# A recurrence-to-expert kernel: constants moved from GpSimd to ScalarE in the opening, more filler matmuls, one bonus product on VectorE

## The chip, the core and the metric

The kernel runs on one core of a Trainium2 chip. The metric is the device time of one execution in microseconds, as the median of several runs. The profile is a separate execution, taken by the hardware profiler; its rows give times from the start of its span. Engines: PE is TensorE (matmul; PEld is its weight load), DVE is VectorE, ACT is ScalarE, POOL is GpSimd, SP is SyncE, which here issues most transfers. TensorE's clock has two levels, 2.4 GHz (shown as a granted clock of 1.00) and 1.2 GHz (0.50).

## What is computed

First a linear recurrence for 4 batches, 8 heads, 768 positions and head size 48, then one of 8 experts for each batch, chosen from the mean of that batch's recurrence output:

```python
for t in range(S):
    cur = einsum('bhd,bhe->bhde', u * k[t], v[t])
    y[t] = einsum('bhd,bhde->bhe', r[t], state + cur)
    state = w * state + einsum('bhd,bhe->bhde', k[t], v[t])
x = y as (B, S, 384)
logits = x.mean(axis=1) @ w_gate ; e = argmax(logits) per batch
out[b] = softmax(logits)[e] * (relu(x[b] @ w1[e]) @ w2[e])
```

## The kernel before

The sequence is cut into 12 blocks of 256 positions, numbered g = 0 to 11, three to a batch. Each block goes through the same steps, and the order of the steps is written out by hand (`manual_schedule`): every engine executes its instructions in the order in which the program text emits them. Two decays are built once from `w` (`dk`, `dr`). For a block, `load(g)` starts three transfers of 384 KB (k, r, v) on SP's queue. `prep_k` and `prep_r` scale k and r by the decays into bf16 (block 0 on VectorE, all others on GpSimd); `prep_v` casts v to bf16 (ScalarE for blocks 0 to 3). `transposes(g, c)` turns k and r round on TensorE in two halves; after each half ScalarE copies the result from PSUM (`kr`, L243) and VectorE forms the product of k and r (`prod`, L244). `scores(g, 0)` and `scores(g, 1)` multiply k with r into one PSUM tile `at`, which VectorE masks into `gt` (L265); there is one buffer of `at`, so the next scores step waits for that masking. `bonus(g)` sums `prod` against the constant `U8` into 16 columns of the PSUM bank `s_ps`, VectorE copies them out (`tcol`, L288), and GpSimd multiplies v by them (`vt`, L296). `scores_v(g, 1, ..)` and `scores_v(g, 0, ..)` multiply `gt` with v into the outputs `ys`, and k with v into the running state in `s_ps`; VectorE then reads that state out with a mask (`st`, L367): with `bmask` after the half-block step, with `wcmask` after the whole block. `inter(g, j)` adds the carried state's part to the output, `add_bonus(g)` adds `vt`, `evac_y(g, j)` lets ScalarE cast the output to `xn` (L380), and `backs(g)` transposes it back (`xp`, L393), sums it over positions into `s_ps` (L397), and ScalarE copies it to `xt` (L401). `outputs(g)` is the run of these from `inter(g, 0)` to `backs(g)`.

The first three blocks (the opening) are ordered one step at a time in the lines from L551 on. After block 2, `pool_sum(0)`, `gate(0)` and `weights(0)` find the expert of batch 0 and GpSimd issues the transfers of its weights (L453, L457). From block 3 on, a loop interleaves the recurrence with jobs of the expert of the batch before (`mm1`, L474, and `mm2`, L494); the first such job comes at the end of block 3. `fill(n, cols)` issues n matmuls on a tile of zeros, whose result nobody reads, and `gap()` is `fill(1, 256)`.

The tile framework adds the waits. For the PSUM bank `s_ps` a later write waits for an earlier read of the same tile. The constants that the change touches are built ahead of all blocks: `wuT` holds w and u by partition (four small transfers on ScalarE's queue, each half filling 48 of 64 partitions); GpSimd squares w eight times (`wpow`, L182) and multiplies the mask by it (`wcmask`, L185), ahead of its scaling of block 1.

Of the kernel before, what the change touches and what calls it, by code (L numbers as in the profile page):

```python
# [9 lines left out]
FP32 = mybir.dt.float32  # L10
FP32R = mybir.dt.float32r
BF16 = mybir.dt.bfloat16
AX = mybir.AxisListType
ALU = mybir.AluOpType
ACT = mybir.ActivationFunctionType
# [3 lines left out]
def kernel(  # L19
# [12 lines left out]
    nc = tc.nc  # L32

    B, H, S, D = r.shape
    DM = H * D
    C = 128
    L = 2 * C
    DP = 64
    NP = H // 2
# [11 lines left out]
    const = ctx.enter_context(tc.tile_pool(name="const", bufs=1))  # L51
    inp = ctx.enter_context(tc.tile_pool(name="inp", bufs=AHEAD))
    work = ctx.enter_context(tc.tile_pool(name="work", bufs=4))
# [18 lines left out]
    def load(g):  # L72
        b, gi = divmod(g, NB)
        for name, src in (("k32", k), ("r32", r), ("v32", v)):
            t = inp.tile([128, H, 2, D], FP32, tag=name, name=f"{name}_{g}")
            nc.sync.dma_start(
                out=t.rearrange("q h c d -> q h (c d)"),
                in_=src[b, :, L * gi : L * gi + L, :].rearrange("h (q c) d -> q h (c d)", c=2),
            )
            raw[name, g] = t  # L80
# [7 lines left out]
    nc.sync.dma_start(out=wrow, in_=w.rearrange("(o h) d -> o (h d)", o=1))  # L88

    wuT = const.tile([128, 2, NP], FP32, tag="wuT", name="wuT")  # L90
    nc.vector.memset(wuT, 0.0)
    with nc.allow_non_contiguous_dma(reason="decay and bonus by partition, 1.5 KB each"):
        for i, src in enumerate((w, u)):
            for a in range(2):
                nc.scalar.dma_start(
                    out=wuT[64 * a : 64 * a + D, i, :],
# [14 lines left out]
    def fill(cnt, cols):  # L111
        for _ in range(cnt):
            nc.tensor.matmul(out=fills[-1][:, 0:cols], lhsT=zero[:, 0:128],  # L113
                             rhs=zero[:, 0:cols], start=True, stop=True)
# [60 lines left out]
    for a in range(2):  # L175
        q = slice(64 * a, 64 * a + 64)
        nc.gpsimd.tensor_mul(
            U8.rearrange("q p h -> q (p h)")[q, a :: H + 2], wuT[q, 1, :], wuT[q, 0, :])
    wpow = [wuT[:, 0, :]]
    while 2 ** (len(wpow) - 1) < L:  # L180
        t = const.tile([128, NP], FP32, tag=f"wpow{len(wpow)}", name=f"wpow{len(wpow)}")
        nc.gpsimd.tensor_mul(t, wpow[-1], wpow[-1])  # L182
        wpow.append(t)
    wcmask = const.tile([128, NP, 2 * D], FP32, tag="wcmask", name="wcmask")
    nc.gpsimd.tensor_mul(  # L185
        wcmask, bmask.rearrange("q p a d -> q p (a d)"),
        wpow[-1].to_broadcast([128, NP, 2 * D]))
    ones_col = const.tile([128, 1], BF16, tag="ones_col", name="ones_col")
    nc.vector.memset(ones_col, 1.0)

# [11 lines left out]
    def prep_k(g):  # L202
        kg, rg = raw.pop(("k32", g)), raw[("r32", g)]
        if g == 0:
            for c in (c0, c1):
                scale(nc.vector, kp[g % NR], kg, dk, c)
                scale(nc.vector, rp[g % NR], rg, dr, c)
        else:
            scale(nc.gpsimd, kp[g % NR], kg, dk, cc)
# [6 lines left out]
    def prep_v(g):  # L216
        vb = work.tile([128, 2, H, D], BF16, tag="vb", name=f"vb{g}")
        vsrc = raw.pop(("v32", g)).rearrange("q h c d -> q c h d")
        if g < NB + 1:
            nc.scalar.copy(vb, vsrc)  # L220
        else:
            nc.gpsimd.tensor_copy(vb, vsrc)
        vbs[g] = vb

    def transposes(g, c):
        if c and g < NB + 2:
            fill_bank()
            twp = pp_moe.tile([128, 2 * NP, 128], BF16, tag="moe", name=f"twp{g}_{c}")
        else:
            twp = pp_tw.tile([128, 2 * NP, 128], BF16, tag="tw", name=f"twp{g}_{c}")  # L230
        for o, src in ((0, kp[g % NR]), (NP, rp[g % NR])):
            for p in range(NP):
                nc.tensor.transpose(  # L233
                    out=twp[:, o + p, :],
                    in_=src[:, c, 2 * p : 2 * p + 2, :].rearrange("s a b -> s (a b)"),
                    identity=ident,
                )
        if c == 0:
            kts[g] = work.tile([128, 2 * NP, 2, 2, 64], BF16, tag="kr", name=f"kr{g}")
            rts[g] = kts[g][:, NP : 2 * NP]  # L240
            prods[g] = work.tile([128, NP, 2, 2, 64], BF16, tag="prod", name=f"prod{g}")
        tw = twp.rearrange("q o (j i) -> q o j i", j=2)
        nc.scalar.copy(kts[g][:, :, :, c, :], tw)  # L243
        nc.vector.tensor_mul(prods[g][:, :, c], tw[:, 0:NP], rts[g][:, :, :, c, :])  # L244

    def scores(g, rnd):
        kt, rt = kts[g], rts[g]
        if rnd == 0:
            gts[g] = work.tile([128, 2, 2, 2, 2, 128], BF16, tag="gt", name=f"gt{g}")
        at = pp_at.tile([128, 2, 2, 2, 128], FP32, tag="at", name=f"at{g}_{rnd}")  # L250
        for pp in range(2):
            p = 2 * rnd + pp
            for cs in range(2):
                for j in range(2):
                    for a in range(2):
                        q = slice(64 * a, 64 * a + D)
                        nc.tensor.matmul(  # L257
                            out=at[64 * j : 64 * j + 64, a, pp, cs, :],
                            lhsT=kt[q, p, j, cs, :],
                            rhs=rt[q, p, j].rearrange("q c i -> q (c i)"),  # L260
                            start=True,
                            stop=True,
                            skip_group_check=True,
                        )
        nc.vector.tensor_mul(  # L265
            gts[g][:, rnd].rearrange("q a p c t -> q (a p) c t"),
            at.rearrange("q a p c t -> q (a p) c t"),
            mask.rearrange("q n s c i -> q n s (c i)"),
        )
# [3 lines left out]
    def bonus(g, now=True):  # L273
        prod = prods[g]
        if g:
            tc_ps = s_ps[(g - 1) // NB][:, TC : TC + 2 * H]
        else:
            tc_ps = pp_y.tile([128, 512], FP32, tag="y0", name="tc0")[:, 0 : 2 * H]
        for c in range(2):
            for p in range(NP):  # L280
                nc.tensor.matmul(
                    out=tc_ps[:, H * c : H * c + H],
                    lhsT=prod[:, p, c].rearrange("q j i -> q (j i)"), rhs=U8[:, p, :],
                    start=(g == 0 and c == 0 and p == 0), stop=(p == NP - 1),
                    skip_group_check=True,
                )
        tcol = work.tile([128, 2 * H], FP32, tag="tcol", name=f"tcol{g}")
        nc.vector.tensor_copy(tcol, tc_ps)  # L288
        tcols[g] = tcol
        if now:  # L290
            vt_mul(g)
# [8 lines left out]
    def inter(g, j):  # L300
        st, rt = sts.pop((g, j)), rts[g]
        yj = ys[g][j]
        for p in range(NP):
            nc.tensor.matmul(  # L304
                out=yj[:, 96 * p : 96 * p + 96],
                lhsT=rt[:, p, j].rearrange("q c i -> q (c i)"), rhs=st[:, p, :],
                start=(j == 0 and p == 0), stop=False, skip_group_check=True,
            )

    def add_bonus(g):  # L310
        vt = vts[g].rearrange("q (c h) d -> q c (h d)", c=2)
        for j, c in ((0, 0), (1, 1), (0, 1), (1, 0)):
            q = slice(64 * j, 64 * j + 64)
            nc.tensor.matmul(  # L314
                out=ys[g][j][64 * c : 64 * c + 64, 0:DM], lhsT=ident[q, q], rhs=vt[q, c, :],
                start=False, stop=True, skip_group_check=True,
            )
# [59 lines left out]
    def evac_y(g, j):  # L377
        if j == 0:
            xns[g] = work.tile([128, 2, DM], BF16, tag="xn", name=f"xn{g}")
        nc.scalar.copy(xns[g][:, j, :], ys[g][j][:, 0:DM])  # L380
# [151 lines left out]
    def outputs(g, gaps=None):  # L532

        gaps = gaps or [lambda: None] * 3
        if g % NB:
            inter(g, 0)
        scores_v(g, 0, g % NB == 0)
        add_bonus(g)
        evac_y(g, 0)
        gaps[0]()  # L540
        inter(g, 1)
        evac_y(g, 1)
        gaps[1]()
        backs(g)
        gaps[2]()

    def gap():
        fill(1, 256)
# [7 lines left out]
    scores(0, 0)  # L556
    prep_v(0)
    load(4)
    fill(5, 512)
    scores(0, 1)  # L560
    bonus(0, False)
# [4 lines left out]
    scores_v(0, 1, True)  # L566
    prep_v(1)
    load(5)
    fill(4, 256)
    scores(1, 0)  # L570
    scores_v(0, 0, True)
    fill(2, 256)
    scores(1, 1)
    bonus(1)
    prep_k(3)
    transposes(2, 0)
    transposes(2, 1)
    prep_v(2)
    add_bonus(0)
    evac_y(0, 0)  # L580
    inter(0, 1)
    evac_y(0, 1)
    gap()
    scores(2, 0)
    scores_v(1, 1, True)
    backs(0)
    gap()
    scores(2, 1)
    bonus(2)
    prep_r(3)  # L590
    outputs(1, [gap] * 3)
    prep_v(3)
    prep_k(4)
    scores_v(2, 1, True)
    outputs(2, [gap] * 3)
    pool_sum(0)
# [92 lines left out]
```

## Time and profile before

| | us |
|---|---|
| median of 3 runs (159.16 to 160.34) | 159.63 |
| the profiled execution, its own time | 161.36 |
| its span, first to last instruction | 159.7 |
| its mean granted TensorE clock | 0.904 |
| PE busy | 146.1 (91%) |
| DVE busy | 74.1 (46%) |
| ACT busy | 82.5 (52%) |
| POOL busy | 72.3 (45%) |

The profiled execution took 161.36 us, of which 1.66 lie outside its span. Busy shares are averages over stages with different limits: the opening lasts until about 37 us, the expert of batch 0 is found and its weights are asked for by 43 us, and its first matmul runs at 52 us. A busy TensorE is not one at its peak, because at 1.2 GHz the same work shows as busy for longer.

### The profile page before, as it was taken

How to read it: one execution, taken by the hardware profiler on the slowest of the kernel's cores; microseconds unless marked ns; L12 is line 12 of the kernel's file. 1: busy time of each engine (PE TensorE's matmuls, PEld its weight loads, DVE VectorE, ACT ScalarE, POOL GpSimd, SP SyncE). 2: the span in 40 equal slices, each digit the busy share in tenths (PEclk: the TensorE clock that was granted, in tenths of full speed). 3: DMA queues.
4: the chain of work that ended last, by engine and by line, in shares of the span. 5: the costliest groups of instructions: out<-in, count | busy, mean ns of one | idle time of the engine just before them, and what ended most of it. 6: DMA issues, size and time to landing. Idle time of an engine off the chain costs nothing.

```text
span 159.7 us, 4549 instructions
## 1 busy us (share of the span) xinstructions
PE 146.1 (91%) x1954; PEld 103.0 (64%) x1954; DVE 74.1 (46%) x164; ACT 82.5 (52%) x138; POOL 72.3 (45%) x72
## 2 busy tenths in 40 slices
PE   6984997798598999999999999999999999999991
PEld 2344676567376787777667877776677765676560
DVE  7863556311655655465545744665274321212110
ACT  1860645255326477654657686553764652265321
POOL 4089944750499492928839193592203020000000
PEclk9998559555559999999999999999999999999999
DMA  3999999700099999999999100299420039970034
GB/s 76 253 261 259 265 234 268 171 4 0 16 233 217 263 255 249 258 272 258 218 222 355 69 4 0 27 208 192 176 99 4 0 43 215 147 290 0 2 141 155
DMA packets 41464, 25.47 MB, mean 160 GB/s; under 512 B 38755, under 2 KB 39012, under 8 KB 41444
## 3 DMA queue, kind: packets, MB, share of 16 engines
q1 hardware_dynamic: 39460, 18.89, 47.3%
q0 software_dynamic: 1152, 6.29, 20.7%
q8 instruction: 15, 0.25, 0.7%
q10 hardware_dynamic: 832, 0.00, 0.3%
q14 instruction: 5, 0.04, 0.1%
HBM read 26.76 MB, written 4.72 MB: 197 GB/s over the span
## 4 chain that ended last, share of the span: by engine, by line
PE 73%; ACT 7%; DVE 6%; POOL 6%; DMA 3%; issue 2%; ACTq 1%; POOLq 1%
PE op L494 20%; PE hp L474 20%; PE twp L233 6%; PE y L344 5%; PE at L257 4%; DMA wuT<-in_u_dram 3%; PE s L352 3%; PE xp L393 3%; ACT kr L243 2%; PE fill L113 2%; POOL rp L196 2%; DVE gt L265 2%; PE y L304 2%; PE y L314 2%; ACT ht L481 2%
## 5 line engine op out<-in xcount | busy, mean ns | idle before, releaser
L474 PE MATMUL hp<-xt,w 128*128 128x384 bf16 x192 | 41.4, 333 | 1.3 <-DVE lg L427 0.3
L243 ACT COPY kr<-twp 128x1024 bf16<-128x1024 bf16 x24 | 24.0, 1012 | 24.1 <-PE twp L233 24.1
L494 PE MATMUL op<-w,ht 128*128 128x384 bf16 x192 | 34.9, 326 | 0.1
L265 DVE TENSOR_TENSOR gt<-at,mask 128x1024 bf16<-128x1024 f32 x24 | 29.3, 1222 | 10.1 <-PE at L257 9.9
L481 ACT ACTIVATE ht<-hp 128x384 bf16<-128x384 f32 x48 | 23.4, 491 | 17.7 <-PE hp L474 17.1
L296 POOL TENSOR_TENSOR vt<-vb,tcol 128x768 bf16<-128x768 bf16 x12 | 17.7, 1477 | 28.2 <-DVE tcol L288 28.2
L474 PEld LDWEIGHTS <-w 128*128 128x128 bf16 x192 | 25.1, 148 | 8.1 <-issue 4.4
L244 DVE TENSOR_TENSOR prod<-twp,kr 128x512 bf16<-128x512 bf16 x24 | 10.2, 425 | 30.9 <-ACT kr L243 30.9
L494 PEld LDWEIGHTS <-ht 128*128 128x128 bf16 x192 | 17.3, 98 | 11.1 <-issue 0.8
L196 POOL TENSOR_TENSOR rp<-r,dr 128x768 bf16<-128x768 f32 x11 | 20.0, 1818 | 0.0
L196 POOL TENSOR_TENSOR kp<-k,dk 128x768 bf16<-128x768 f32 x11 | 20.0, 1815 | 0.0
L113 PE MATMUL fill<-zero 128*128 128x256 bf16 (+1 forms) x48 | 15.6, 432 | 1.3 <-DVE zero L85 1.3
L344 PEld LDWEIGHTS <-gt 64*128 64x128 bf16 x384 | 12.6, 98 | 6.0 <-issue 5.1
L501 ACT ACTIVATE ob<-op,gw 128x384 f32<-128x384 f32 x16 | 9.3, 581 | 13.1 <-PE op L494 12.9
L344 PE MATMUL y<-vb,gt 64*128 64x48 bf16 x384 | 15.3, 188 | 0.6 <-ACT xn L380 0.6
L380 ACT CAST xn<-y 128x384 bf16<-128x384 f32 x24 | 11.3, 480 | 5.9 <-PE y L314 4.9
L483 DVE TENSOR_SCALAR ht<-hp 128x384 bf16<-128x384 f32 x16 | 8.9, 554 | 11.7 <-PE hp L474 11.5
L257 PE MATMUL at<-kr 48*64 48x128 bf16 x384 | 11.1, 240 | 3.0 <-ACT kr L243 1.5
L453 POOL DMA_DIRECT2D w<-in_moe_w_dram x4 | 2.5, 623 | 22.9 <-DVE gw L443 8.3
L257 PEld LDWEIGHTS <-kr 48*64 48x64 bf16 x384 | 7.6, 116 | 7.9 <-issue 6.6
L233 PE MATMUL twp<-ident,rp 128*128 128x128 bf16 x96 | 11.2, 250 | 1.4 <-POOL rp L196 1.4
L352 PE MATMUL s<-vb,kp 64*128 64x96 bf16 x160 | 11.7, 222 | 0.8 <-DVE tcol L288 0.8
(72 smaller groups left out, 162.8 us busy)
## 6 DMA issues: line engine op xcount, KB each, us to landing
w<-in_moe_w_dram POOLq DMA_DIRECT2D x8, 768.0 KB, 9.8
k<-in_k_dram SPq DMA_DIRECT2D x12, 384.0 KB, 6.2
r<-in_r_dram SPq DMA_DIRECT2D x12, 384.0 KB, 6.4
v<-in_v_dram SPq DMA_DIRECT2D x12, 384.0 KB, 6.3
out_dram<-ob SPq DMA_DIRECT2D x11, 384.0 KB, 4.8
out_dram<-ob SPq DMA_DIRECT2D x2, 192.0 KB, 1.9
wuT<-in_w_dram ACTq DMA_DIRECT2D x2, 0.8 KB, 3.6
wuT<-in_u_dram ACTq DMA_DIRECT2D x2, 0.8 KB, 4.7
```

Source lines behind the costliest of these rows:

```text
L113: nc.tensor.matmul(out=fills[-1][:, 0:cols], lhsT=zero[:, 0:128], rhs=zero[:, 0:cols], start=True, stop=True)
L196: eng.tensor_mul(dst[:, cs, :, 0:D].rearrange("q c h d -> q h c d"), src[:, :, cs, :], dec[:, :, cs, :])
L233: nc.tensor.transpose(out=twp[:, o + p, :], in_=src[:, c, 2 * p : 2 * p + 2, :].rearrange("s a b -> s (a b)"), identity=ident,)
L243: nc.scalar.copy(kts[g][:, :, :, c, :], tw)
L257: nc.tensor.matmul(out=at[64 * j : 64 * j + 64, a, pp, cs, :], lhsT=kt[q, p, j, cs, :], rhs=rt[q, p, j].rearrange("q c i -> q (c i)"), sta ...
L265: nc.vector.tensor_mul(gts[g][:, rnd].rearrange("q a p c t -> q (a p) c t"), at.rearrange("q a p c t -> q (a p) c t"), mask.rearrange("q n ...
L296: nc.gpsimd.tensor_mul(vt, vbs[g].rearrange("q c h d -> q (c h) d"), tcol.to_broadcast([128, 2 * H, D]))
L344: nc.tensor.matmul(out=yj[:, D * h : D * h + D], lhsT=gt[q, p // 2, a, p % 2, c, :], rhs=vb[q, c, h, :], start=(first and i == 0), stop=(c ...
L352: nc.tensor.matmul(out=sp[:, 96 * p : 96 * p + 96], lhsT=kp[g % NR][qo, c, 2 * p : 2 * p + 2, :].rearrange("s a b -> s (a b)"), rhs=vb[qo, ...
L474: nc.tensor.matmul(out=hp[:, 0:SB], lhsT=w1[:, ct, ft::NFT], rhs=xts[b][:, ct, SB * sb : SB * sb + SB], start=(ct == 0), stop=(ct == NCT - 1),
L481: nc.scalar.activation(out=o, in_=hp[:, 0:SB], func=ACT.Relu)
L494: nc.tensor.matmul(out=op[:, 0:DM], lhsT=ht[:, ft, 128 * si : 128 * si + 128], rhs=w2[:, ft, :], start=(ft == 0), stop=(ft == NFT - 1),)
```

## The change

The eight squarings and the masked product leave GpSimd. ScalarE computes w to the power 256 as exp(256 ln w) with two small activations in the place of the squarings, and writes `wcmask` with four scaled copies after it has cast v of block 0. The unused partitions of `wuT` are filled with 0.5 in place of 0, so that the logarithm stays finite. `bonus(g, None)` is a new form: VectorE multiplies v by the sums straight from PSUM, with no `tcol` and no work on GpSimd; block 2 uses it. The order of the opening changes: the first half of the transposes of block 2 comes ahead of `scores(1, 1)`; the outputs of block 1 are spread round `scores(2, 1)` and come ahead of `bonus(2)`; fillers are of other counts and widths, and most of the gaps leave.

```diff
-    nc.vector.memset(wuT, 0.0)
+    nc.vector.memset(wuT, 0.5)
...
-    wpow = [wuT[:, 0, :]]
-    while 2 ** (len(wpow) - 1) < L:
-        t = const.tile([128, NP], FP32, tag=f"wpow{len(wpow)}", name=f"wpow{len(wpow)}")
-        nc.gpsimd.tensor_mul(t, wpow[-1], wpow[-1])
-        wpow.append(t)
+    lnwT = const.tile([128, NP], FP32, tag="lnwT", name="lnwT")
+    nc.scalar.activation(out=lnwT, in_=wuT[:, 0, :], func=ACT.Ln)
+    wcT = const.tile([128, NP], FP32, tag="wcT", name="wcT")
+    nc.scalar.activation(out=wcT, in_=lnwT, func=ACT.Exp, scale=float(L))
     wcmask = const.tile([128, NP, 2 * D], FP32, tag="wcmask", name="wcmask")
-    nc.gpsimd.tensor_mul(
-        wcmask, bmask.rearrange("q p a d -> q p (a d)"),
-        wpow[-1].to_broadcast([128, NP, 2 * D]))
+
+    def late_constants():
+        for p in range(NP):
+            nc.scalar.activation(
+                out=wcmask[:, p, :], in_=bmask[:, p].rearrange("q a d -> q (a d)"),
+                func=ACT.Copy, scale=wcT[:, p : p + 1])
...
+        if now is None:
+            vts[g] = work.tile([128, 2 * H, D], BF16, tag="vt", name=f"vt{g}")
+            nc.vector.tensor_mul(
+                vts[g], vbs[g].rearrange("q c h d -> q (c h) d"),
+                tc_ps.to_broadcast([128, 2 * H, D]))
+            return
         tcol = work.tile([128, 2 * H], FP32, tag="tcol", name=f"tcol{g}")
...
     load(4)
+    late_constants()
     fill(5, 512)
...
     load(5)
-    fill(4, 256)
+    fill(3, 512)
     scores(1, 0)
     scores_v(0, 0, True)
-    fill(2, 256)
+    transposes(2, 0)
+    fill(1, 512)
     scores(1, 1)
     bonus(1)
     prep_k(3)
-    transposes(2, 0)
     transposes(2, 1)
     prep_v(2)
+    fill(2, 512)
     add_bonus(0)
     evac_y(0, 0)
     inter(0, 1)
     evac_y(0, 1)
-    gap()
     scores(2, 0)
     scores_v(1, 1, True)
     backs(0)
     gap()
+    inter(1, 0)
+    scores_v(1, 0, False)
     scores(2, 1)
-    bonus(2)
+    add_bonus(1)
+    evac_y(1, 0)
+    inter(1, 1)
+    evac_y(1, 1)
+    bonus(2, None)
     prep_r(3)
-    outputs(1, [gap] * 3)
     prep_v(3)
     prep_k(4)
+    backs(1)
+    gap()
     scores_v(2, 1, True)
```

## Rows read from the trace of the kernel before

**Rows 1.** Five stretches of TensorE: length, busy (instructions), granted clock, DMA share, GB/s.

```profile
12.40:15.10 2.70, 0.70 (x15) 0.87 1.28 259
15.10:24.60 9.50, 9.41 (x148) 0.50 1.17 250
25.50:28.05 2.55, 2.35 (x66) 1.00 1.19 289
28.05:48.50 20.45, 17.31 (x226) 0.50 0.40 88
52.10:159.70 107.60, 102.57 (x1356) 1.00 0.63 153
```

**Rows 2.** The chain that ended last, parts: start, length, what.

```profile
8.48 0.21 POOL wpow L182
...
10.69 0.79 POOL wcmask L185
...
15.10 1.46 PE twp L233 x12
...
52.14 0.64 PE hp L474 x3
```

**Rows 3.** Timeline of POOL: start, length, what, idle time before it.

```profile
13.24 1.80 POOL L196 TENSOR_TENSOR rp<-r,dr 128x768 bf16<-128x768 f32 x1
...
16.76 1.82 POOL L196 TENSOR_TENSOR rp<-r,dr 128x768 bf16<-128x768 f32 x1
18.54 1.48 POOL L296 TENSOR_TENSOR vt<-vb,tcol 128x768 bf16<-128x768 bf16 x1
...
42.24 0.72 POOL L453 DMA_DIRECT2D w<-in_moe_w_dram x1 [8.26 <-DVE gw L443]
```

**Rows 4.** DMA issues at 5.10, 9.66, 10.13; last column, us to landing.

```profile
r<-in_r_dram SPq DMA_DIRECT2D x1, 384.0 KB, 6.3
...
k<-in_k_dram SPq DMA_DIRECT2D x1, 384.0 KB, 4.9
...
r<-in_r_dram SPq DMA_DIRECT2D x1, 384.0 KB, 5.9
```

**Rows 5.** Timeline of ACT: two pairs of copies and the nearest small activation.

```profile
8.28 1.93 ACT L243 COPY kr<-twp 128x1024 bf16<-128x1024 bf16 x2 [0.74 <-PE twp L233]
...
15.74 1.93 ACT L243 COPY kr<-twp 128x1024 bf16<-128x1024 bf16 x2 [4.81 <-PE twp L233]
...
40.73 0.30 ACT L439 ACTIVATE exps<-lg,negmax 128x8 f32<-128x8 f32 x1 [1.09 <-DVE negmax L437]
```

**Rows 6.** Groups by form, 4 to 60 us: count, busy us, mean ns, idle before.

```profile
L265 DVE TENSOR_TENSOR gt<-at,mask 128x1024 bf16<-128x1024 f32 x11 | 13.5, 1224 | 4.1 <-PE at L257 4.0
...
L296 POOL TENSOR_TENSOR vt<-vb,tcol 128x768 bf16<-128x768 bf16 x5 | 7.4, 1475 | 7.9 <-DVE tcol L288 7.9
...
L244 DVE TENSOR_TENSOR prod<-twp,kr 128x512 bf16<-128x512 bf16 x12 | 5.1, 425 | 15.1 <-ACT kr L243 15.1
...
L380 ACT CAST xn<-y 128x384 bf16<-128x384 f32 x10 | 4.6, 484 | 4.7 <-PE y L314 4.4 <-PE y L304 0.3
...
L367 DVE TENSOR_TENSOR st<-s,wcmask 128x384 bf16<-128x384 f32 x4 | 2.2, 550 | 0.9 <-PE s L352 0.9
```

**Rows 7.** Timeline of PE: two scores steps, one at the other clock, two state steps.

```profile
18.21 0.64 PE L257 MATMUL at<-kr 48*64 48x128 bf16 x16
...
24.02 0.64 PE L257 MATMUL at<-kr 48*64 48x128 bf16 x16
...
27.06 0.42 PE L257 MATMUL at<-kr 48*64 48x128 bf16 x16
...
28.89 0.24 PE L352 MATMUL s<-vb,kp 64*128 64x96 bf16 x1 [0.81 <-DVE tcol L288]
...
32.04 0.53 PE L333 MATMUL s<-st,ident 128*128 128x384 bf16 x1
```

## The prediction

> **What bounds the kernel now.** I read the stretches of TensorE first. From 52.1 us to the end TensorE is busy 102.57 of 107.6 us at the full clock [rows 1]: that part is a fixed amount of matmul work, and nothing in the diff touches it. So the question is how much earlier this part starts. Ahead of it TensorE runs at 1.2 GHz for two long stretches, 15.1 to 24.6 and 28.05 to 48.5 [rows 1]. The first comes behind a stretch in which it was busy for only 0.70 of 2.70 us; the second behind one with 2.35 of 2.55 busy. So one fall follows a starved engine, and the other does not.
>
> Then the chain of waits says what starved it: GpSimd squares from 8.48, ends `wcmask` at 11.48 [rows 2], and only then scales block 1; the second half of that, rp of block 1, ends at 15.04 [rows 3], and TensorE's 12 transposes start at 15.10 [rows 2]. At the far end of the opening the chain passes block 2's state step (carry at 32.04 [rows 7]), the issue of the weights at 42.24 [rows 3] and the first expert matmul at 52.14 [rows 2]. Carry to issue is 10.2 us, issue to first expert matmul 9.9 us. What the change is worth is how much earlier the carry of block 2 comes, and at which clock the stretch behind it runs.
>
> **The change part by part.** *GpSimd's constants.* From 8.48 to 11.48 is 3.00 us gone. Block 1's scaling then waits for its data. r of block 1 landed at 5.10 + 6.3 = 11.4 [rows 4]; k of block 1 was queued one transfer earlier, 393 KB at 259 GB/s [rows 1] or 1.5 us, so I estimate its landing at 9.9. kp runs 9.95 to 11.75 and rp, at 1.80 each [rows 3], to 13.55 in place of 15.04: a gain of 1.5. Bounds: if k landed as late as r did, kp starts at 11.45 and there is no gain; if it landed before 9.6, rp is held by r itself, 11.4 + 1.8 = 13.2, a gain of 1.85. Block 2 is tighter: k landed at 9.66 + 4.9 = 14.55, r at 10.13 + 5.9 = 16.05 [rows 4], so kp runs 14.6 to 16.4, rp to 18.2 in place of 18.58 [rows 3]. Of the 3.0 us, 0.4 is left there, and the bonus product of block 0 behind it ends at 19.7 in place of 20.0.
>
> *The same constants on ScalarE.* The logarithm and the exponential, about 0.30 each [rows 5], fall into 0.74 us of idle time ahead of the first pair of copies; bounds 0 to 0.3 on that pair, and TensorE's next wait, for rp at 13.55, takes up 0.3. The four scaled copies have 96 columns each, between 0.30 (8 columns) and 0.48 (384 columns) [rows 5, 6], so 1.2 to 1.9 us in 4.81 us of idle time: nothing. Were that cover gone, they would delay the copies of block 1 one for one.
>
> *TensorE to S(1,0)* (S for a scores step). The last transposes of block 1 start at 13.6. ScalarE's pair of copies takes 1.93 [rows 5] and follows 0.4 behind: 14.0 to 15.95. The new fillers, 3 x 512 columns, are 0.65 us at 2.4 GHz and end by 15.6, so S(1,0) starts at 16.0 in place of 18.21 [rows 7], 2.2 earlier. At 1.2 GHz the three are 1.3 us (the four that leave were 0.85) and S(1,0) starts at 17.1.
>
> *S(1,1) and S(2,0).* The first transposes of block 2 now stand ahead of S(1,1), and everything queued behind them on TensorE waits for rp of block 2 at 18.2: TensorE idles about 1 us there. They end at 18.6, one copy of 0.97 ends at 19.65, `prod` (0.425 [rows 6]) at 20.1, and on VectorE the masking of S(1,1) stands behind `prod`: 20.1 to 21.3 (1.224 [rows 6]). S(2,0) needs that buffer: 21.35 in place of 24.02 [rows 7], 2.7 earlier. The 2 x 512 fillers (0.43) lie in that wait. At 1.2 GHz S(2,0) starts at 22.5.
>
> *Block 1's outputs and the bonus on VectorE.* ScalarE's queue is copy to 20.9, cast of v, then the two casts of block 0's output (0.484 each [rows 6]) to 22.45. The state step of block 1 runs 22.5 to 23.05, `st` reads the bank to 23.65 (0.55 [rows 6]), and the second state step follows at 24.25. Before, it stood behind the `tcol` copy and started at 28.89 [rows 7]; now it is ahead of `bonus(2)`, and that wait is gone. A wait takes its place further on: the sums at L397 in `backs(1)`, and the carry of block 2 behind them, write to the bank that VectorE reads while it forms `vt`. The trace has no such product from PSUM. From below, `prod` (bf16 on both sides) scaled to 768 columns is 0.64 us; from above, GpSimd's own product is 1.475 [rows 6]. The nearest row is the masking with a 4-byte PSUM operand: between its 1.224 for 1024 columns and the 0.55 of `st` for 384 lie 1.05 ns a column, so 0.95 us. GpSimd is no bound here: block 1's `vt` is 21.4 + 1.475 = 22.9, ahead of its use at 26. On ScalarE the cast of v of block 3 now stands ahead of the copy to `xt` of block 1, as long as one `vb` cast; the bank that this copy frees is wanted some 3 us later, so it is hidden.
>
> Here the PSUM wait can be weighed against a page. The row shows a state matmul at 28.89 waiting 0.81 us for a copy of other columns of the same bank [rows 7]. The Trainium skill, "PSUM — Partial Sum Buffer", section "PSUM bank collisions raise a hardware error", says to guard PSUM by bank and quadrant, "not by address", so a longer read on VectorE is a longer lock on TensorE; the trace agrees with 0.81 us. By addresses alone the carry below would come at 27.85; by the row it comes at 28.2, which I use.
>
> *The clock and the carry.* With the 2.0 us of pause from 12.4 to 15.1 [rows 1] cut to some 0.6 (the wait for rp until 13.6), I expect the clock to survive that stretch. The stretch from 21 to 25 has pauses of 0.6 (for the masking), 0.5 (for the casts) and 0.2, with little filler in them, and the second fall before came from only 0.2 us of pause in 2.55 [rows 1]. So I put a fall near 24.6. From there at 1.2 GHz: state step to 25.0, S(2,1) to 25.6 (0.64 in place of 0.42 [rows 7]), `st` to 25.6, masking to 26.9, `vt` to 27.75, L397 to 28.1, carry at 28.2 in place of 32.04 [rows 7]: **3.85 earlier**. The steps from carry to weights and on to the first expert matmul are the same instructions at the same clock, so the issue comes at 38.4 and the first expert matmul at 48.3. Loads of blocks 6 to 8 stand behind a fence on the gate and move with it. A fall at 28 as before gives 4.2, at 21.2 3.2, at 18 2.2.
>
> The sum against the profiled execution is 161.36 - 3.85 = 157.5 us. That execution was 1.73 above the median of the runs shown, so against the median it is 159.63 - 3.85 = **155.8 us**.
>
> **The rivals.** *The clock holds to the gate.* Carry at 27.85, then state steps, casts and back-transposes at 2.4 GHz: sums at 31.1, weights at 35.3, 6.9 us earlier, 152.7 us. For it: no pause in the new order exceeds about 1 us. The Trainium skill, "TensorE: Matmul & The Clock Gate", Part 1, has "the default state is throttled, and activity releases the throttle"; by that rule alone pauses so short would keep it open, and the time is this rival's 152.7. Against it: the clock fell at 28.05 behind a stretch 92% busy [rows 1].
>
> *The first fall stays.* If k of block 1 lands late, or the new fillers do not hold the clock, everything from 14.5 on runs at 1.2 GHz. Then the same pass gives S(1,0) 17.1, S(2,0) 23.5, carry about 31.1: 0.9 earlier, 158.7 us. This is also the case in which the change does not do what it says, because the loads, not GpSimd, hold blocks 1 and 2.
>
> *Slower.* The first fall stays, and the clock that came back at 48.5 [rows 1], 3.6 us ahead of the first expert matmul, comes back behind it. Dense expert work at half the clock loses half of its time. With 0.9 gained, it is slower than before once more than 1.8 us of expert work run at 1.2 GHz; 6 us of it cost 3.0, net 2.1, 161.7 us. Against it: that stage's instructions are unchanged.
>
> **How the numbers follow.** Forecast (a later fall, 2.2 to 4.2 earlier) 0.55; clock held 0.17; first fall stays 0.18; slower 0.05; 0.05 for no change. One per cent, 1.6 us, is about what a measurement here tells from no change. Faster by more takes the forecast, the held clock and a few of the first-fall cases: 0.80; within 1%: 0.15; slower: 0.05. The range runs from the held clock with 0.7 more, for the bounds of rp and `vt` (152.0), to 0.6 gained (159.0).
>
> **What would show it.** Right: no GpSimd work between 8.5 and 9.9; rp of block 1 done near 13.55 and of block 2 near 18.2; granted clock 1.00 past 15; S(2,0) near 21.4; `vt` of block 2 on VectorE near 0.95 us with L397 waiting for it; carry near 28.2; weights at 38.4. Wrong: a granted clock of 0.50 from 15 on (too fast a forecast), or 1.00 until the gate (too slow).

## The result and the profile after

The changed kernel takes 155.21 us (median of 4 executions, 154.31 to 156.05) against 159.99 for the kernel before; the ratio is 0.9705, 95% interval 0.9616 to 0.9794. The forecast was 155.8. Its four executions stand in two pairs: 154.31 and 154.39, with a mean granted clock of 0.978 and 0.975, and 156.04 and 156.05, both with 0.941. The median lies between the pairs, where no execution lies. The profiled one is the first, with a span of 152.6 us. (Medians here are over all executions of a kernel and ratios over those within about 1.5% of its fastest, so where the executions spread widely the two can differ.)

TensorE by stretch in the changed kernel; the columns are those of [rows 1]:

```profile
12.40:15.10 2.70, 2.56 (x67) 1.00 1.16 321
15.10:24.60 9.50, 7.71 (x198) 1.00 1.05 281
24.60:28.00 3.40, 2.45 (x54) 1.00 0.77 205
28.00:34.40 6.40, 4.40 (x65) 1.00 0.01 2
34.40:41.30 6.90, 5.42 (x85) 0.51 0.73 158
45.10:152.60 107.50, 102.54 (x1355) 1.00 0.60 153
```

Read the last row first. From the first expert matmul to the end TensorE is busy 102.54 of 107.50 us; before it was 102.57 of 107.60 [rows 1]. So all of the profiled difference, 159.7 - 152.6 = 7.1 us, lies ahead of that matmul (52.1 before, 45.1 now). In the stretch from 12.4 to 15.1 TensorE is busy 2.56 us where it was 0.70, and the granted clock stays at 1.00 until 34.4, where it was 0.50 from 15.1 to 24.6 and from 28.05 to 48.5. The last column holds something that the prediction did not have: the loads run at 321 GB/s, against 259 [rows 1].

POOL in the changed kernel, timeline (start, length, what, idle time before it and what ended it):

```profile
9.16 1.81 POOL L199 TENSOR_TENSOR kp<-k,dk 128x768 bf16<-128x768 f32 x1 [1.44 <-DMA k<-in_k_dram]
10.92 1.82 POOL L199 TENSOR_TENSOR rp<-r,dr 128x768 bf16<-128x768 f32 x1
...
14.52 1.82 POOL L199 TENSOR_TENSOR rp<-r,dr 128x768 bf16<-128x768 f32 x1
...
35.32 0.72 POOL L462 DMA_DIRECT2D w<-in_moe_w_dram  x1 [7.78 <-DVE gw L452]
```

Against [rows 3]: rp of block 1 ends at 12.74 instead of 15.04, rp of block 2 at 16.34 instead of 18.58, and the weights are issued at 35.32 instead of 42.24. ScalarE and VectorE in the changed kernel, timelines:

```profile
7.44 0.19 ACT L180 ACTIVATE lnwT<-wuT 128x4 f32<-128x4 f32 x1
7.67 0.20 ACT L182 ACTIVATE wcT<-lnwT 128x4 f32<-128x4 f32 x1
8.77 1.93 ACT L246 COPY kr<-twp 128x1024 bf16<-128x1024 bf16 x2 [0.90 <-PE twp L236]
...
11.32 1.18 ACT L187 ACTIVATE wcmask<-bmask,wcT 128x96 f32<-128x96 f32 x4
13.88 1.93 ACT L246 COPY kr<-twp 128x1024 bf16<-128x1024 bf16 x2 [1.39 <-PE twp L236]
```

```profile
24.58 1.22 DVE L268 TENSOR_TENSOR gt<-at,mask 128x1024 bf16<-128x1024 f32 x1
25.71 0.94 DVE L292 TENSOR_TENSOR vt<-vb,s 128x768 bf16<-128x768 bf16 x1
```

The moved constants cost nothing: 0.9 us of idle time is left behind the two small activations and 1.39 behind the four copies. TensorE in the changed kernel, timeline (two scores steps, the sums of block 1 and the carry of block 2):

```profile
15.86 0.42 PE L260 MATMUL at<-kr 48*64 48x128 bf16 x16 [0.31 <-ACT kr L246]
...
20.67 0.42 PE L260 MATMUL at<-kr 48*64 48x128 bf16 x16 [0.47 <-DVE tcol L297]
...
26.71 0.29 PE L406 MATMUL s<-ones_col,xn 128*128 128x1 bf16 x6 [0.80 <-DVE vt L292]
26.98 0.32 PE L342 MATMUL s<-st,ident 128*128 128x384 bf16 x1
```

S(1,0) starts at 15.86, S(2,0) at 20.67, the carry of block 2 at 26.98; before these were 18.21, 24.02 and 32.04 [rows 7]. The row at 26.71 is the new wait: the sums stand 0.80 us for the product that VectorE reads out of the same bank.

### The profile page after: what moved, and what is told of

It is laid out like the page before. It is cut to its first block, busy times and chain, and to the rows that moved or that the text cites. A ratio compares the mean times of both kernels' runs of the same rounds, so it can differ in the third digit from the quotient of the medians.

```text
span 152.6 us, 4539 instructions
## 1 busy us (share of the span) xinstructions
PE 139.5 (91%) x1951; PEld 97.9 (64%) x1951; DVE 74.4 (49%) x164; ACT 83.6 (55%) x144; POOL 68.5 (45%) x62
## 4 chain that ended last, share of the span: by engine, by line
PE 78%; DVE 10%; ACT 8%; issue 2%; DVEq 0%
PE op L503 21%; PE hp L483 21%; PE twp L236 7%; PE at L260 5%; DVE gt L268 5%; PE fill L113 5%; PE y L353 5%; ACT kr L246 4%; PE s L361 2%; PE xp L402 2%; ACT ht L490 2%; PE y L313 2%; PE y L323 2%; DVE ht L492 1%; DVE st L376 1%
## 5 line engine op out<-in xcount | busy, mean ns | idle before, releaser
L305 POOL TENSOR_TENSOR vt<-vb,tcol 128x768 bf16<-128x768 bf16 x11 | 16.3, 1477 | 25.4 <-DVE tcol L297 25.4
L113 PE MATMUL fill<-zero 128*128 128x512 bf16 (+1 forms) x45 | 14.5, 430 | 1.9 <-DVE zero L85 1.3
L353 PEld LDWEIGHTS <-gt 64*128 64x128 bf16 x384 | 11.5, 94 | 5.0 <-issue 3.9
L492 DVE TENSOR_SCALAR ht<-hp 128x384 bf16<-128x384 f32 x16 | 8.9, 554 | 11.7 <-PE hp L483 11.5
L353 PE MATMUL y<-vb,gt 64*128 64x48 bf16 x384 | 14.1, 182 | 0.4 <-ACT xn L389 0.4
L260 PE MATMUL at<-kr 48*64 48x128 bf16 x384 | 10.5, 229 | 3.6 <-ACT kr L246 1.7
L260 PEld LDWEIGHTS <-kr 48*64 48x64 bf16 x384 | 7.0, 110 | 8.2 <-issue 6.2
L410 ACT COPY xt<-xp 128x768 bf16<-128x768 bf16 x12 | 9.6, 798 | 4.3 <-PE xp L402 4.3
L361 PE MATMUL s<-vb,kp 64*128 64x96 bf16 x160 | 10.5, 208 | 0.4 <-DVE st L376 0.4
```

Source lines behind the costliest of these rows:

```text
L260: nc.tensor.matmul(out=at[64 * j : 64 * j + 64, a, pp, cs, :], lhsT=kt[q, p, j, cs, :], rhs=rt[q, p, j].rearrange("q c i -> q (c i)"), sta ...
L305: nc.gpsimd.tensor_mul(vt, vbs[g].rearrange("q c h d -> q (c h) d"), tcol.to_broadcast([128, 2 * H, D]))
L353: nc.tensor.matmul(out=yj[:, D * h : D * h + D], lhsT=gt[q, p // 2, a, p % 2, c, :], rhs=vb[q, c, h, :], start=(first and i == 0), stop=(c ...
L361: nc.tensor.matmul(out=sp[:, 96 * p : 96 * p + 96], lhsT=kp[g % NR][qo, c, 2 * p : 2 * p + 2, :].rearrange("s a b -> s (a b)"), rhs=vb[qo, ...
```

## The experiments

Kernels of one group ran on one chip, beside its own runs of the kernel before: the first four below (before: median 160.09), the next four (160.38) and the last four (160.80).

| kernel | median us | lowest to highest | ratio to before, interval |
|---|---|---|---|
| before_again | 160.44 | 158.61 to 161.79 | 1.0043 (0.9977 to 1.0109) |
| const_only | 157.91 | 156.61 to 158.98 | 0.9949 (0.9884 to 1.0014) |
| order_only | 158.43 | 156.17 to 160.00 | 0.9964 (0.9908 to 1.0020) |
| small_fills | 155.35 | 154.22 to 156.54 | 0.9792 (0.9649 to 0.9935) |
| after_again | 154.55 | 154.20 to 155.75 | 0.9663 (0.9607 to 0.9719) |
| before_shifted | 159.66 | 158.37 to 160.29 | 0.9967 (0.9925 to 1.0009) |
| after_shifted | 155.65 | 155.41 to 156.18 | 0.9725 (0.9676 to 0.9774) |
| bonus_pool | 153.48 | 153.06 to 153.65 | 0.9585 (0.9538 to 0.9632) |
| no_fills | 157.16 | 154.63 to 157.41 | 0.9700 (0.9596 to 0.9805) |
| more_fills | 154.89 | 154.53 to 156.38 | 0.9701 (0.9631 to 0.9771) |
| gate_first | 154.10 | 153.19 to 156.13 | 0.9618 (0.9550 to 0.9686) |
| both | 152.37 | 152.00 to 153.12 | 0.9530 (0.9470 to 0.9590) |

### The halves of the change

*before_again*, with no edit:

> The kernel before, once more, for a second trace of it. Theory A (the gain is GpSimd's 3 us and, through it, a clock that no longer falls): the same two falls of the granted clock near 14.5 and 28, mean clock near 0.90, time 159 to 160.5 us. Rival D (the transfers of this profile were slow, and the pause before rp of block 1 is a matter of the loads): loads near 320 GB/s instead of 260 and a time below 158 us.

It came out at the kernel before's own time, with loads at 261 GB/s at 8.5 to 11.5 us. So the slow loads belong to the kernel, not to one profile, and the rival that laid them on that profile falls. The first fall of theory A did not come near 14.5: TensorE starves here too (busy 1.24 of 2.70 us from 12.4 to 15.1), but the granted clock reads 1.00 there, 0.82 over 15.1 to 24.6 and 0.50 over 28 to 37. This execution took 160.20 us at a mean clock of 0.925. The profile behind [rows 1], 161.36 us at 0.904, is of the slowest kind: only the four slowest of these twelve executions (161.37 to 161.79) have 0.904.

*const_only*: the kernel before with the constants' lines of the diff alone. *order_only*: the changed kernel with those lines taken back.

> The kernel before with only the constants moved to ScalarE; order, fillers and the bonus product as before. Theory A: rp of block 1 ends 1.5 to 2.3 us earlier, the pause at 12.4 to 15.1 shrinks, the first fall goes away in most executions and the time drops by 1 to 3 us, to 157 to 158.5. Rival B (the new order does it, GpSimd's constants were covered by the loads): within 0.5 us of before.

> The changed kernel with the constants back on GpSimd; new order, new fillers and the product on VectorE kept. Theory A: the pause ahead of rp of block 1 returns, the granted clock falls near 14.5 again and about 0.9 to 2 us of the 4.8 us are left, 157.5 to 159 us. Rival B: nearly all of the gain stays, 155 to 156 us.

By medians the constants alone are worth 2.2 us (160.09 to 157.91) and the order alone 1.7 (158.43). Their ratios leave both open, since each interval reaches past 1; the executions of the kernel before lie between 157.32 and 161.49 in that group. Neither half alone comes near the whole: the changed kernel is 160.38 - 154.55 = 5.8 below before in its own group, against 2.2 + 1.7 = 3.9. So rival B, that the order does it and nearly all of the gain stays, falls. In the two traces, TensorE by stretch (const_only, then order_only):

```profile
8.50:11.50 3.00, 2.31 (x33) 1.00 1.17 321
12.40:15.10 2.70, 2.61 (x68) 1.00 1.17 325
15.10:24.60 9.50, 6.59 (x154) 0.88 1.05 281
24.60:28.00 3.40, 2.79 (x59) 0.50 0.70 192
```

```profile
8.50:11.50 3.00, 3.00 (x33) 1.00 1.28 261
12.40:15.10 2.70, 1.23 (x31) 1.00 1.29 260
15.10:24.60 9.50, 7.74 (x182) 1.00 1.13 246
28.00:37.00 9.00, 6.11 (x116) 1.00 0.35 89
```

Where the constants are off GpSimd the pause is gone (2.61 of 2.70 us busy), and where they are on it TensorE starves again (1.23). That is the prediction's first step. Its second, that the pause makes the clock fall, these rows do not show: in order_only the clock reads 1.00 behind the starved stretch and on to 37 us, and in const_only, with no pause, it is down to 0.50 from 24.6 on. The trace of order_only is of its fastest execution (156.17 us at 0.975); nine of its twelve have a mean clock of 0.923 to 0.935, and no trace shows where it fell in those. By median the mean clock is 0.935 in the kernel before, 0.940 in const_only, 0.933 in order_only and 0.970 over the ten executions of the changed kernel. So the clock comes up clearly only with both halves together; that this is the part of the gain that the halves do not add up to is likely, but not shown. The last column holds another difference: 321 GB/s in const_only against 261 in order_only, though nothing in the diff touches a load.

### Why the loads became faster

The eight `wpow` tiles and the two that replace them lie in the same pool as all constants, ahead of the input tiles. Each takes 32 bytes per partition, so the input tiles moved down by 6 x 32 = 192 bytes, from 52672 to 52480, which is a multiple of 256. (The addresses are those of the program's allocation; no trace shows them.) Two kernels part this from the work on GpSimd. Each adds one constant that nobody reads:

```diff
 before_shifted
+    pad = const.tile([128, 16], FP32, tag="pad", name="pad")
+    nc.vector.memset(pad[:, 0:1], 0.0)
 after_shifted
+    pad = const.tile([128, 48], FP32, tag="pad", name="pad")
+    nc.vector.memset(pad[:, 0:1], 0.0)
```

> The kernel before with one unused constant of 64 bytes per partition, so that the input tiles start at 52736, a multiple of 256 bytes, in place of 52672 (192 past one); nothing else. Theory L (the loads' rate follows the start address of the tiles): 315 to 325 GB/s at 8.5 to 11.5 us in place of 261, with the squarings still on GpSimd; rp of block 1 stays near 14.9 because GpSimd is busy until 11.3; time within 1 us of before. Rival G (GpSimd's small operations slow the transfers): 261 GB/s as before.

> The changed kernel with one unused constant of 192 bytes per partition, so that the input tiles start at 52672 as in the kernel before. Theory L: loads at 261 GB/s; kp of block 1 starts near 9.95 and rp of block 2 ends near 18.2, as the prediction had it, TensorE idles 1 us ahead of scores(1, 1), and the time is 0.5 to 1.5 us above the changed kernel. Rival G: 321 GB/s as in the changed kernel and its time.

TensorE by stretch in before_shifted, then in after_shifted; look at the last column:

```profile
8.50:11.50 3.00, 2.85 (x33) 1.00 1.17 317
12.40:15.10 2.70, 1.40 (x36) 1.00 1.17 324
```

```profile
8.50:11.50 3.00, 2.52 (x33) 1.00 1.28 261
12.40:15.10 2.70, 2.31 (x65) 1.00 1.29 259
```

The rate follows the address in both directions and GpSimd's squarings in neither: 317 GB/s with the squarings running, 261 without them. Three start addresses were tried, two of them multiples of 256. The pause follows the work on GpSimd and not the rate: TensorE is busy 1.40 of 2.70 us with the constants on GpSimd and fast loads, 2.31 with them off it and slow loads. The Trainium skill, "DMA: Bandwidth & Descriptors", section "How a descriptor splits into AXI transactions", says that a transaction must start at a 256-byte boundary, so that a descriptor which starts elsewhere spends beats on bytes that it does not use. It says so of reads, and here the moved end is the written one. By its rule as an estimate, two rows of 384 bytes need 12 + 16 beats from a multiple of 256 and 18 + 14 from 192 past one, a ratio of 0.875; the runs show 261 / 321 = 0.81. Direction and order of size agree; that beats are the cause was not measured.

What the rate is worth depends on who waits for the loads. In before_shifted GpSimd is busy with constants until 11.0, and the time stays (0.9967, interval 0.9925 to 1.0009). With the constants gone it is 1.1 us, 155.65 against 154.55 in the same group; executions of the two at the same mean clock (0.974 to 0.975) differ by 0.9 to 1.2. POOL in after_shifted, timeline:

```profile
10.09 1.82 POOL L201 TENSOR_TENSOR kp<-k,dk 128x768 bf16<-128x768 f32 x1 [1.31 <-DMA k<-in_k_dram]
11.86 1.82 POOL L201 TENSOR_TENSOR rp<-r,dr 128x768 bf16<-128x768 f32 x1
14.59 1.81 POOL L201 TENSOR_TENSOR kp<-k,dk 128x768 bf16<-128x768 f32 x1 [0.91 <-DMA k<-in_k_dram]
16.36 1.81 POOL L201 TENSOR_TENSOR rp<-r,dr 128x768 bf16<-128x768 f32 x1
```

This is the kernel that the prediction had worked out: kp of block 1 at 10.09 (9.95 predicted), rp of block 2 done at 18.17 (18.2). Its later steps too: S(1,0) at 16.15 (16.0), S(2,0) at 21.41 (21.35), carry at 27.71 (27.85 by the pass at full clock). The clock falls only behind the carry (0.59 over 28 to 37), so the weights come at 36.88, between the forecast's 38.4 and the 35.3 of the rival in which the clock holds. Against the trace of order_only, which has the same slow loads and a clock that holds as well until then, the carry is 0.77 us earlier (27.71 against 28.48): by these two traces GpSimd's constants alone are worth so much at this clock and rate.

### The product on VectorE

*bonus_pool*:

```diff
-    bonus(2, None)
+    bonus(2)
```

> The changed kernel with the bonus product of block 2 as before: copied out by VectorE, multiplied on GpSimd. Prediction's step: the bank is free 0.8 us earlier (0.165 for the copy in place of 0.94 for the product), so the carry of block 2 comes 0.8 us earlier; vt on GpSimd ends near 27.4 to 28.8, ahead of or beside its use by add_bonus of block 2 at 28.5. Theory V (the product on VectorE is worth something): 0.3 to 1 us slower than the changed kernel because vt is late. Rival W (it costs more on the bank than it saves): 0.3 to 0.8 us faster.

It is 1.07 us faster than the changed kernel of the same group (153.48 against 154.55), and its six executions (to 153.65) lie below all six of the other (from 154.20). TensorE in bonus_pool, timeline:

```profile
25.75 0.30 PE L406 MATMUL s<-ones_col,xn 128*128 128x1 bf16 x6
26.01 0.32 PE L342 MATMUL s<-st,ident 128*128 128x384 bf16 x1
```

The row of the sums has no wait. The carry comes at 26.01 instead of 26.79 in that group's trace of the changed kernel, 0.78 earlier, which is the difference of the two reads, 0.94 - 0.165 = 0.78. GpSimd forms `vt` from 25.84 to 27.31 and its use starts near 27.6, so the product that was moved was not late where it had been. This part of the change is a loss: rival W, not theory V, and by more than the 0.3 to 0.8 us that W had. The trace shows 0.78 of the 1.07; the rest was not traced.

### The fillers

*small_fills* takes the counts of before, *no_fills* leaves out what lies between block 1's transposes and block 2's outputs, *more_fills* adds some:

```diff
 small_fills
-    fill(3, 512)
+    fill(4, 256)
...
-    fill(1, 512)
+    fill(2, 256)
...
-    fill(2, 512)
 no_fills
-    fill(3, 512)
...
-    fill(1, 512)
...
-    fill(2, 512)
...
-    gap()
...
-    gap()
 more_fills
+    fill(2, 512)
     scores(2, 0)
...
-    gap()
+    fill(2, 512)
     inter(1, 0)
```

> The changed kernel with the filler columns of before (four and two of 256, the two of 512 ahead of the bonus of block 0 left out): 1536 columns fewer. If the fillers hold the clock (theory A), it falls between 14 and 22 us and the time goes to 156 to 158.5 us. Rival C (the clock is held by the work that is no longer starved, fillers are padding): the same times as the changed kernel, 154.3 to 156.1, or 0.3 us less.

> The changed kernel without any filler between the transposes of block 1 and the outputs of block 2 (3072 columns of 512 and two gaps of 256 left out). If the fillers hold the clock: the granted clock falls to 0.50 between 14 and 25 us in most executions and the time is 156.5 to 158.5 us. If the work that is no longer starved holds it: the clock stays at 1.00 to about 28 and the time is 154 to 155 us.

> The changed kernel with two more fillers of 512 columns ahead of scores(2, 0) and two in place of the one of 256 behind backs(0). If the executions above 155.5 us are those whose clock falls between 17 and 28 us, these go away and all lie within 154.0 to 155.0. If the fillers are on the path there, all are 0.3 to 0.6 us longer than the changed kernel.

Without fillers four of six executions take 157.15 to 157.41, one 155.61 and one 154.63. The trace is of one of the four; TensorE by stretch in no_fills:

```profile
12.40:17.40 5.00, 3.41 (x107) 1.00 1.16 321
17.40:20.90 3.50, 3.48 (x48) 0.51 0.91 231
20.90:24.20 3.30, 2.13 (x59) 1.00 1.17 320
24.20:44.70 20.50, 17.85 (x264) 0.50 0.41 96
```

The clock falls behind 5.0 us with 3.41 busy, comes back, and falls again behind 3.3 with 2.13 busy; then it stays low for 20.5 us. So the fillers hold the clock in most executions, and one execution out of six got by without them. With the columns of before (small_fills) three executions take 154.22 to 154.62 and three 156.08 to 156.54: half and half, as in the first four of the changed kernel. Its trace is of one of the short ones, 154.62 us, although the clock was low for a time there too (0.83 over 15.1 to 24.6, then 0.97 to 28). So a fall that is soon made good costs little. Whether the changed kernel itself comes in two kinds, after_again was to show:

> The changed kernel once more, to see how its executions spread. Theory A2 (the clock's later fall comes in some executions only): times in two groups, near 154.3 with a mean clock near 0.98 and near 156.1 with 0.94. Rival: one group, and the spread of the first four was chance.

Five lie within 154.20 to 154.76, at mean clocks of 0.955 to 0.978, and one at 155.75, at 0.953: these are not the two groups of theory A2. With more fillers five lie within 154.53 to 155.28 and one at 156.38: the long executions did not go away, and there is no gain. What parts the long ones from the short ones is shown only by a neighbour, gate_first below, whose trace is of an execution of 156.12 us with a mean clock of 0.942. TensorE by stretch in gate_first:

```profile
24.60:27.20 2.60, 1.65 (x33) 1.00 0.75 191
27.20:44.20 17.00, 14.58 (x205) 0.50 0.50 98
```

There the clock falls at 27.2, just behind the carry of block 2 (26.81); the prediction had put such a fall at 24.6, ahead of the carry. In the two traces of the changed kernel it falls at 34.4 (154.31 us) and at 33.0 (after_again, 154.76): the later it falls, the shorter the execution.

### What was late next

*gate_first*, and *both*, which has the edit of bonus_pool as well:

```diff
     pool_sum(0)
-    transposes(3, 0)
     gate(0)
     weights(0)
+    transposes(3, 0)
```

> The changed kernel with the gate and the weights of batch 0 ahead of the first transposes of block 3. In the changed kernel the copy of the logits on VectorE stands behind prod of block 3, which waits for ScalarE's copy, and the second copy of block 3 stands behind the exponential of the gate. Without that the logits are copied near 31.4 in place of 33.1, the weights are issued near 33.6 in place of 35.3, scores(3, 0) starts near 33.7 in place of 35.06, and the time drops by 1.2 to 1.7 us. Rival: block 3 bounds that stage by itself, and the gain is under 0.4 us.

> The bonus product of block 2 back on GpSimd and the gate ahead of block 3's transposes. If the two gains are on the same path one after the other, they add: 154.6 - 1.1 - 1.4, about 152.1 us. If the late vt of block 2 on GpSimd holds rp of block 3, and with it the transposes, the sum is less: 153 us.

gate_first is 0.45 below after_again by median (154.10 and 154.55, in different groups), with two of seven executions at 156.1: less than the 1.2 to 1.7 expected, and near the rival's 0.4. In its trace the clock is at 0.50 from 27.2 on, so the expected steps cannot be read there. both takes 152.37 us, ratio 0.9530, the best of all; that is nearer to 152.1, where the gains add, than to 153, but four of its six executions have a mean clock of 0.989, which bonus_pool never has. VectorE in both, timeline:

```profile
30.48 0.17 DVE L436 COPY lg<-lgp 128x8 f32<-128x8 f32 x1 [0.93 <-PE lgp L431]
...
31.99 0.43 DVE L247 TENSOR_TENSOR prod<-twp,kr 128x512 bf16<-128x512 bf16 x1 [0.86 <-ACT kr L246]
32.33 0.14 DVE L446 TENSOR_SCALAR negmax<-top 128x1 f32<-128x1 f32 x1
```

Compared with the trace of bonus_pool, the logits are copied 1.64 us earlier (30.48 against 32.12) and the weights issued 1.64 earlier (32.72 against 34.36), as expected. The first expert matmul gains only 0.66 (43.54 against 44.20). The rows show what holds it: the first step of the gate's weight (`negmax`) still stands behind `prod` of block 3, the exponential waits for it (ScalarE, 32.51), and ScalarE's second copy of block 3 stands behind the exponential (32.72), so S(3,0) moves only from 34.10 to 33.76. Putting `gate_weight` elsewhere was not tried.

## Why the prediction was right in its time, and what failed in its steps

- **GpSimd's constants make the pause, and their new place costs nothing: right.** The pause goes and comes with them, in const_only and order_only and at either rate of the loads (before_shifted, after_shifted). ScalarE's four copies took 1.18 us (1.2 to 1.9 predicted), the logarithm and the exponential 0.19 and 0.20 (0.30).
- **The pause as what brings the first fall: not shown.** Only the profile of the kernel before has that fall. Before_again, before_shifted and order_only starve in the same stretch (1.23 to 1.40 of 2.70 us busy) and read 1.00 past it, and const_only falls without a pause. Moving the constants does go with a higher clock in the new order: 0.923 to 0.935 in nine of twelve executions of order_only, 0.956 or more in all six of after_shifted, at the same rate of the loads. By which step is open.
- **"Block 2 is tighter ... 0.4 is left there": wrong for this kernel.** The step took the landing times of the kernel before. The change moved the input tiles by 192 bytes, the loads went from 261 to 321 GB/s, and rp of block 2 came 2.24 earlier instead of 0.4. With the tiles put back (after_shifted) the step holds, 18.17 against 18.2. The term that the sum had at nothing measured 1.1 us.
- **The scores steps: right in kind.** S(1,0) came at 15.86 (16.0), but by another limit: rp of block 1 was done at 12.74, and the transposes start at 13.24 behind TensorE's own work, without a wait. S(2,0) came at 20.67 (21.35); the 0.7 at S(2,0) is the loads', since it starts at 21.41 in after_shifted.
- **The product on VectorE: sized right, 0.94 us against 0.95, and so was its wait.** The text had it as the wait that takes the place of the one removed, but did not set it against leaving the product on GpSimd. bonus_pool does: without it the kernel is 1.07 us faster.
- **"So I put a fall near 24.6": wrong for the profiled execution.** The clock held to 34.4, the carry came at 26.98 and the weights at 35.32; the rival "the clock holds to the gate" had 35.3 for them and 6.9 us, and this execution is 161.36 - 154.31 = 7.05 below the profiled one of before. The two executions at 156.05, 3.9 below the 159.99 of before, come near the forecast's 3.85, at a lower mean clock; no trace of one of these was taken. In gate_first's, of an execution as long, the fall came behind the carry and not ahead of it. So the median lies between the forecast and that rival.
- **Right time, in part by luck.** Two errors made the forecast too slow: the 1.1 us of the loads, and a clock that fell ahead of the carry, where in both traces of the changed kernel it held to 33.0 or longer. One made it too fast: the gain was worked out from an execution of the slowest kind, with the carry at 32.04, and taken off the median, while in before_again's execution of 160.20 us the carry comes at 30.89, so that 1.15 of the 3.85 us were not there to gain. And 155.21 is the middle of two pairs; in after_again the median is 154.55, a gain of 5.8 us in that group.
- **"The first fall stays" and the slower rival** did not come true in any of the ten executions of the changed kernel: none took longer than 156.05. Without the fillers four of six take about 157.2, and the one that was traced has a fall at 17.4.

What stays open is what decides in which executions the clock falls, and whether the pause has a part in it; more fillers did not settle it, and no low-clock execution of order_only was traced.

## What to carry to other kernels

A tile that is added or removed moves all tiles behind it: before crediting an edit with a faster load, compare GB/s in the same stretch, and try an unused pad on both kernels. When VectorE is made to read a product's operand straight from PSUM, price the time for which the bank is held, not the instruction: a 0.165 us copy freed it 0.78 us sooner than a 0.94 us product did. Where the clock of TensorE rides on an opening full of waits, one profile is one sample: run the kernel often enough to see how its executions spread before a gain of one per cent is believed, and see where the profiled execution lies among them before its waits are priced.

## What the runs showed of the hardware that was not expected

Loads in rows of 384 bytes into tiles that start at a multiple of 256 bytes ran at 317 GB/s (before_shifted) and 321 (the changed kernel) from 8.5 to 11.5 us, and at 261 when the tiles started 192 bytes past one, with the same transfers and in both kernels. One program, unchanged, gave executions of different clocks: 154.31 us at a mean of 0.978 and 156.05 at 0.941. And a starved stretch (1.23 of 2.70 us busy) was followed by a granted clock of 1.00 for over 20 us in one kernel (order_only), while a kernel without it (const_only) fell to 0.50 ahead of 24.6.
